# The first batch's last 64 queries as one step of their own, among the first group's products

## The chip, the cores and the metric

The kernel runs on one core of a Trainium2 chip. The metric is the device time of one execution in microseconds (us); the profiles are of one execution each, taken by the hardware profiler. Engines are named as in the profile: PE is TensorE's matrix multiplication, PEld its weight loads, DVE is VectorE, ACT ScalarE, POOL GpSimd, and SP issues most DMAs. TensorE has two clock levels, 1.2 and 2.4 GHz; the granted clock 1.00 in a row is the higher one.

## What is computed

Four batches of 8 heads with 576 queries and keys of width 64 go through attention in a causal window of 128 keys with a linear distance bias. The 2304 result rows go through a gated layer of width 1536, and then through 8 experts of width 1024, of which each row takes its best two by noisy logits. The core of the reference, cut:

```python
scores = scale * q @ k.T;  mask = (rel >= 0) & (rel < 128)
attn = softmax(where(mask, scores - slope[h] * abs(rel), -1e9)) @ v
g = x @ w_gate;  x = (silu(g) * (x @ w_val)) @ w_out
noisy = x @ g_w + log1p(exp(x @ n_w)) * noise      # best two of 8, softmax over the two
out[mask] += weight * (relu(x[mask] @ w1[e]) @ w2[e])
```

The weights of the gated layer come as 64-bit floats.

## The kernel before

**Order of the whole.** The attention of batch 0 runs first, alone. Then come four groups of result rows, `GRP`: rows 0 to 511, then 640, 512 and 640. For each group the gated layer (`mlp1`) is written as a list of pieces, `hidden` (12 blocks of 128 hidden units, two matrices, in halves) and `rows` (the product with `w_out`), and the attention of the next batch and small work on the last group (`post`) as a second list `side`. `merge(a, b, lead, late)` deals the second list evenly among the first, not before `late` pieces and not in the last `lead`. At the end come the routing (`route`) and the 8 experts.

**Who orders.** The instructions of each engine are put in order by a planner that simulates the program as written; within an engine they run in that order, each waiting for its semaphores. For DVE and POOL the first part of the program (until the sixth piece of the attention of batch 0) keeps the written order. So what is written later can be moved ahead: the conversion of the first weights (`Convert.one`, lines 224 to 238: ACT L232 and L233, DVE L234 and L235, a store to DRAM and the next load on SP) and their split into two rounded parts (ACT L280, DVE L281) lie between batch 0's attention. At most three split tiles (`wu`) and three converted ones (`wst`) can lie ready.

**Three products for one.** Every product of the gated layer is three matrix multiplications of rounded parts (`three`, L306 to L308). Its moving operand is `xT`, the attention result of a batch, channels on partitions.

**Group borders.** Batch 0 has 576 queries and group 0 takes 512 of them. The result of the last 64 goes to the tile `hold` and is copied in front of batch 1's result when batch 1's attention begins (`first`, L523). So it isn't needed before the second group.

**Attention of a pair of heads** (`pair_items`). Queries are cut into 9 blocks of 64. `tr` transposes q and k (`"t"`: the last 64 of both) and copies them to `qT` and `kT`; a score unit is one block of queries against up to 192 keys for two heads, 64 partitions each. In batch 0 (`qk1`, L427) q is laid out with zeros so that one multiplication over 128 rows gives both heads; the q copies are cut by head between ACT (L384) and DVE (L382), a call holds two units, and there are five calls. In the other batches (`qk4`, L444) four 64x64 tiles of TensorE work at once: two heads, two lanes of blocks; the second lane has its heads swapped on the partitions, and needs the bias table `tabs[1]`, which is `tabs[0]` shifted by 64 partitions. `softmax` adds the bias and takes the minimum of the negated scores (DVE L405), exponentiates (ACT L408), sums and inverts (L409, L410) and multiplies (POOL L417 in batch 0, DVE L415 in the others). `pt` transposes the probabilities (L461) and copies them (ACT L464 to L468, half-height ones on DVE L479 in batch 0). `pv` multiplies by v (L491) and writes the result in two rounded parts (ACT L507, DVE L508). The keys of `todo` give the order of a pair's pieces, and `z` shifts the pairs against each other.

**Buffers.** In batch 0 pairs 0 and 2 use one set (`SET[0]`), pairs 1 and 3 another that lies where the gated layer's hidden tiles come later. The other batches use `SET[0]` alone. Score banks are two, taken in turn by `qk1`.

**Constants.** `late_consts` (L646) issues `tabs[1]` on POOL and loads the routing weights and the noise on SP. It stands in front of the first group's products.

```python
bias(0)
...
late_consts()
...
    if b == 0:
        hidden.insert(3, lambda: (load_qk(1, 0), load_v(1, 0)))
```

## Time and profile before

| | us |
|---|---|
| median of 3 runs | 1104.43 (1102.92 to 1106.14) |
| the profiled execution | 1104.11 |
| its span, first to last instruction | 1102.0 |
| TensorE busy in the span | 1063.7 (97%) |
| DVE, ACT, POOL busy | 563.7, 476.4, 326.5 |
| mean granted clock | 0.987 |

A row that groups instructions reads: line, engine, operation, what is written from what, shapes, count, then busy us, mean ns of one, then idle time of the engine before them and what ended it. Instructions of one engine overlap at their ends, so a sum of durations can be over the time that passed; the distance from one start to the next is what counts there.

### The profile page before, as it was taken

The page shows a single profiled execution, that of the slowest core. Times are in us where ns is not written, and L with a number is a line of the kernel's source. Part 1 is how long each engine was busy: PE and PEld are TensorE (multiplying, and loading weights), DVE is VectorE, ACT ScalarE, POOL GpSimd, SP SyncE. Part 2 cuts the span into 40 slices and gives each one's busy share as a digit, 9 for nine tenths or more (in the row PEclk, how much of TensorE's full clock was granted, in tenths as well). Part 3 has the DMA queues.
Part 4 walks back from the last instruction along what each step waited for, and adds up shares of the span by engine and source line. Part 5 has one row for each costly group of instructions (what it writes and reads, how often), then busy time and mean ns, then how long its engine had stood idle before and what let it go on. Part 6 is the DMA issues. An engine that isn't in the chain of part 4 may idle for free. (4 is left out here: it accounts for less than half of the span.)

```text
span 1102.0 us, 17616 instructions
## 1 busy us (share of the span) xinstructions
PE 1063.7 (97%) x6694; PEld 909.1 (82%) x6694; DVE 563.7 (51%) x1267; ACT 476.4 (43%) x1093; POOL 326.5 (30%) x324
## 2 busy tenths in 40 slices
PE   6789999999999999999999999999999999999996
PEld 4457778799988777788998887988989898989894
DVE  6869972577640476325885355534343434343321
ACT  6868864566541456445543233423232323232210
POOL 5110003122223433142368324414141314141301
PEclk9889999999999999999999999999999999999998
DMA  8867664233362323241322415635353534443201
GB/s 208 224 202 236 218 223 154 73 91 90 101 231 82 122 86 110 71 153 39 99 96 96 153 40 165 201 113 174 105 173 105 173 115 153 136 154 115 71 27 42
DMA packets 124207, 143.87 MB, mean 131 GB/s; under 512 B 66062, under 2 KB 94766, under 8 KB 124112
## 3 DMA queue, kind: packets, MB, share of 16 engines
q1 hardware_dynamic: 112464, 108.88, 32.0%
q0 software_dynamic: 10448, 33.47, 9.1%
q8 instruction: 55, 0.90, 0.3%
q10 hardware_dynamic: 1200, 0.30, 0.1%
q14 instruction: 40, 0.33, 0.1%
HBM read 113.84 MB, written 28.91 MB: 130 GB/s over the span
## 5 line engine op out<-in xcount | busy, mean ns | idle before, releaser
L281 POOL TENSOR_TENSOR wu<-wst,wu 128x1024 fp32r<-128x1024 f32 x54 | 130.0, 2410 | 360.4 <-ACT wu L280 360.4
L910 PE MATMUL b<-xT,wu 128*128 128x304 f32 (+2 forms) x1536 | 221.4, 303 | 0.0
L910 PEld LDWEIGHTS b<-xT,wu 128*128 128x128 f32 x1536 | 216.5, 188 | 2.3 <-DVE xT L898 0.3
L306 PE MATMUL b<-xT,wu 128*128 128x320 f32 (+1 forms) x576 | 199.3, 350 | 0.8 <-ACT xT L507 0.8
L307 PE MATMUL b<-xT,wu 128*128 128x320 f32 (+1 forms) x576 | 196.2, 341 | 0.0
L308 PE MATMUL b<-xT,wu 128*128 128x320 f32 (+1 forms) x576 | 195.9, 341 | 0.0
L306 PE MATMUL b<-wu,hTa 128*128 128x512 f32 (+1 forms) x482 | 191.5, 400 | 0.2 <-DVE sg L590 0.2
L307 PE MATMUL b<-wu,hTa 128*128 128x512 f32 (+1 forms) x482 | 188.8, 392 | 0.0
L308 PE MATMUL b<-wu,hTa 128*128 128x512 f32 (+1 forms) x482 | 187.3, 392 | 0.0
L280 ACT ACTIVATE wu<-wst 128x1024 fp32r<-128x1024 f32 x136 | 143.6, 1058 | 95.4 <-PE b L308 72.1
L281 DVE TENSOR_TENSOR wu<-wst,wu 128x1024 fp32r<-128x1024 f32 x82 | 100.3, 1224 | 37.7 <-ACT wu L280 35.1
L306 PEld LDWEIGHTS b<-xT,wu 128*128 128x128 f32 x576 | 108.0, 189 | 13.4 <-issue 3.3
L917 DVE SCALAR_TENSOR_TENSOR hTa<-b,hTa 128x304 fp32r<-128x304 f32 (+2 forms) x128 | 56.8, 470 | 117.4 <-ACT hTa L916 101.4
L307 PEld LDWEIGHTS b<-xT,wu 128*128 128x128 f32 x576 | 108.5, 188 | 9.2 <-issue 1.7
L308 PEld LDWEIGHTS b<-xT,wu 128*128 128x128 f32 x576 | 108.5, 188 | 8.7 <-issue 1.5
L916 ACT ACTIVATE hTa<-b 128x304 fp32r<-128x304 f32 (+2 forms) x128 | 50.3, 422 | 145.6 <-PE b L910 140.0
L308 PEld LDWEIGHTS b<-wu,hTa 128*128 128x128 f32 (+1 forms) x482 | 88.9, 184 | 21.0 <-issue 0.3
L306 PEld LDWEIGHTS b<-wu,hTa 128*128 128x128 f32 (+1 forms) x482 | 88.8, 184 | 19.6 <-issue 1.5
L307 PEld LDWEIGHTS b<-wu,hTa 128*128 128x128 f32 (+1 forms) x482 | 89.0, 185 | 18.4 <-issue 0.2
L887 POOL DMA_INDIRECT xo<-x2d,gib x37 | 36.2, 980 | 174.4 <-PE b L894 164.0
L897 ACT ACTIVATE xT<-b 128x512 fp32r<-128x512 f32 (+1 forms) x40 | 22.9, 574 | 142.0 <-PE b L894 142.0
L592 DVE TENSOR_TENSOR hTa<-sg,hTa 128x320 fp32r<-128x320 f32 (+1 forms) x54 | 66.7, 1239 | 24.3 <-ACT hTa L591 24.3
(198 smaller groups left out, 1297.1 us busy)
## 6 DMA issues: line engine op xcount, KB each, us to landing
wst<-in_moe_w_dram SPq DMA_DIRECT2D x64, 512.0 KB, 3.7
wst<-wscr SPq DMA_DIRECT2D x54, 512.0 KB, 3.2
wscr<-wst SPq DMA_DIRECT2D x18, 512.0 KB, 3.1
cs<-in_moe_w_gate_dram SPq DMA_DIRECT2D x12, 512.0 KB, 4.8
cs<-in_moe_w_val_dram SPq DMA_DIRECT2D x12, 512.0 KB, 6.8
cs<-in_moe_w_out_dram SPq DMA_DIRECT2D x12, 512.0 KB, 5.7
x2d<-xT POOLq DMA_DIRECT2D x18, 256.0 KB
out_dram<-sg SPq DMA_DIRECT2D x1, 4608.0 KB, 15.6
```

Source lines behind the costliest of these rows:

```text
L280: nc.scalar.activation(o[0], s, AF.Copy)
L281: self.eng(n).tensor_sub(o[1], s, f32(o[0]))
L306: nc.tensor.matmul(ps, st(0), mv(0), start=first, stop=False, skip_group_check=True)
L307: nc.tensor.matmul(ps, st(0), mv(1), start=False, stop=False, skip_group_check=True)
L308: nc.tensor.matmul(ps, st(1), mv(0), start=False, stop=last, skip_group_check=True)
L592: nc.vector.tensor_sub(hh(1, f, sl), t, f32(hh(0, f, sl)))
L887: nc.gpsimd.indirect_dma_start(out=x[0:r], out_offset=None, in_=x2d[0:GRP[-1][0], :] if (e, g) == (0, False) else x2d, in_offset=bass.Indi ...
L897: nc.scalar.activation(d[0], tv, AF.Copy)
L910: nc.tensor.matmul(ps[g][:, 0:hi - lo], w[:, a, c * 128:(c + 1) * 128], xgt(e, m, g)[:, c, 0:hi - lo], start=(c == 0 and a + m == 0), stop ...
L916: nc.scalar.activation(d, ps[g][:, 0:hi - lo], AF.Relu)
L917: nc.vector.scalar_tensor_tensor(h2[1][:, f, lo:hi], ps[g][:, 0:hi - lo], 0.0, f32(d), op0=OP.max, op1=OP.subtract)
```

## The change

In batch 0 the pairs leave out block 8. The 64-row loads of q, k and v go, and the pieces `tr("t")`, the unit of block 8, `pt(4)` and the last part of the second `pv`. The eight other blocks go through `qk4` in two calls a pair, as in the other batches; the q layout with zeros, its memsets and the copies cut by head go. `tabs[1]` is therefore brought pair by pair, behind each call of `bias` (`swapped`, six POOL DMAs instead of two).

A new function `last` does block 8 for all 8 heads. It loads the last 64 queries, their 192 keys and values for all heads (five DMAs on SP), into `SET[0]`'s q, k and v tiles. `tr` transposes, `qk` makes 8 score products (two tiles at once), one `softmax` call takes four units with the multiplication on DVE, `pt` transposes the probabilities and copies them into the q and k tiles, and `pv` accumulates into one bank and writes `hold`. Its load is inserted in the pieces of the first group's products, its four steps stand first in `side`, then batch 1's first loads, `late_consts` and two empty entries; the side work begins after 6 pieces and not after 8.

```diff
+    def swapped(lo, hi):
+        for o in (0, QB):
+            nc.gpsimd.dma_start(tabs[1][o:o + QB, lo:hi], tabs[0][QB - o:128 - o, lo:hi])
+
     bias(0)
+    swapped(0, 1)
 
     def load_nat(t, src, b, p, rest=None):
 
         eng = nc.scalar if src is k and (b, p) == (0, 0) else nc.sync
         for i in range(2):
             eng.dma_start(t[:, 0:4, i, :], src[b, 2 * p + i, 0:512, :].rearrange("(i p) d -> p i d", p=128))
-        eng.dma_start(t[0:64, 4] if rest is None else rest, src[b, 2 * p:2 * p + 2, 512:576, :].rearrange("h p d -> p h d"))
+        if b:
+            eng.dma_start(t[0:64, 4] if rest is None else rest, src[b, 2 * p:2 * p + 2, 512:576, :].rearrange("h p d -> p h d"))
...
-                self.qt = self.r[:, 0:NQ * 128]
-
-            qv = self.qt.rearrange("p (j c) -> p j c", c=128)
-            nc.gpsimd.memset(qv[0:64, :, 64:128], 0.0)
-            nc.gpsimd.memset(qv[64:128, :, 0:64], 0.0)
...
-    PVS = [[(0, 0, 256, 0), (1, 0, 128, 128)],
-           [(1, 128, 128, 0), (2, 0, 256, 0), (3, 0, 192, 128), (4, 0, 64, 256)]]
+    def pvs(b, half):
+        if half == 0:
+            return [(0, 0, 256, 0), (1, 0, 128, 128)]
+        return [(1, 128, 128, 0), (2, 0, 256, 0)] + ([(3, 0, 192, 128), (4, 0, 64, 256)] if b else [(3, 0, 128, 128)])
...
+    def softmax(units, eng):
+
+
+        nu = len(units)
+        mn = att.tile([128, 5], F32, name="mn", bufs=4)
+        sm = att.tile([128, 5], F32, name="sm", bufs=4)
+        for i, (x, ps, tab) in enumerate(units):
+            nc.vector.tensor_tensor_reduce(x, ps, tab, op0=OP.add, op1=OP.min, scale=1.0, scalar=3e38,
+                                           accum_out=mn[:, i:i + 1])
+            nc.scalar.activation(x, x, AF.Exp, scale=-1.0, bias=mn[:, i:i + 1], accum_out=sm[:, i:i + 1])
+        nc.vector.tensor_scalar(sm[:, :nu], sm[:, :nu], 1e-9, None, op0=OP.add)
+        nc.vector.reciprocal(sm[:, :nu], sm[:, :nu])
+        for i, (x, _, _) in enumerate(units):
+            eng.tensor_scalar(x, x, sm[:, i:i + 1], 1.0, op0=OP.mult, op1=OP.mult)
...
+                                g, _, _, c = place(j)
+                                units.append((j % 8, (bf.s[g][:, c:c + w], ps[sw][:, po[sw]:po[sw] + w],
+                                                      tabs[sw][:, p, 192 - w:])))
                                 po[sw] += w
                     in_order(mm)
-                    softmax(sorted(units, key=lambda u: u[0] % 8))
+                    softmax([u for _, u in sorted(units, key=lambda u: u[0])], nc.vector if b else nc.gpsimd)
...
                     bias(p)
-
-            rest = lambda: (tr("t")(), nxt(load_qk))
+                    swapped(1, 2)
+
+            rest = lambda: (b and tr("t")(), nxt(load_qk))
             v0 = lambda: (vp(), pt(0)())
             if b == 0:
                 z = (0, 3, 7, 10)[p]
-                todo = [(0, first), (1, tr("k")), (2, rest), (3, qk1(0)), (4, qk1(1)), (5, qk1(2)), (6, v0), (7, qk1(3)),
-                        (7, pt(1)), (8, qk1(4)), (9, pv(0)), (10, pt(2)), (11, pt(3)), (12, pt(4)), (13, pv(1))]
+                todo = [(0, first), (1, tr("k")), (2, rest), (3, qk4((0, 1), (2, 3))), (5, qk4((4, 5), (6, 7))), (6, v0),
+                        (7, pt(1)), (9, pv(0)), (10, pt(2)), (11, pt(3)), (13, pv(1))]
...
+    def last(bk):
+
+        st = {}
+        bf = SET[0]
+
+        def load():
+            st["q"], st["k"] = bf.nat("qn"), bf.nat("kn")
+            t, m = slice(512, S), slice(384, 512)
+            for o, src, sl in ((st["q"][0:64], q, t), (st["q"][64:128], k, t), (st["k"], k, m), (bf.v[0], v, m),
+                               (bf.v[1][0:64], v, t)):
+                nc.sync.dma_start(o[:, 0:HP].rearrange("s p h d -> s (p h) d"), src[0, :, sl, :].rearrange("h s d -> s h d"))
+
+        def tr():
+            t = bk.get("t"), bk.get("t")
+            for i, src in enumerate((st["q"], st["k"])):
+                for p in range(HP):
+                    nc.tensor.transpose(t[i][:, p * 128:(p + 1) * 128], src[:, p].rearrange("s h d -> s (h d)"), ident)
+            t = [x.rearrange("c (p s) -> c p s", p=HP) for x in t]
+            st["qt"] = bf.qt[:, 0:256].rearrange("c (p s) -> c p s", p=HP)
+            st["kt"] = bf.qt[:, 256:1024].rearrange("c (p s) -> c p s", p=HP)
+            nc.scalar.activation(st["qt"], t[0][:, :, 0:64], AF.Copy, scale=-1.0 / math.sqrt(D))
+            nc.scalar.activation(st["kt"][:, :, 128:192], t[0][:, :, 64:128], AF.Copy)
+            nc.scalar.activation(st["kt"][:, :, 0:128], t[1], AF.Copy)
+
+        def x(p):
+            return bf.s[p // 2][:, p % 2 * 192:p % 2 * 192 + 192]
+
+        def qk():
+            ps = bk.get("s"), bk.get("s")
+            o = [ps[p // 2][:, p % 2 * 192:p % 2 * 192 + 192] for p in range(HP)]
+            for p in range(HP):
+                for h in range(2):
+                    hr = slice(64 * h, 64 * h + 64)
+                    nc.tensor.matmul(o[p][hr], st["qt"][hr, p], st["kt"][hr, p], start=True, stop=True, skip_group_check=True)
+            softmax([(x(p), o[p], tabs[0][:, p, :]) for p in range(HP)], nc.vector)
+
+        def pt():
+            t = bk.get("t"), bk.get("t")
+            for p in range(HP):
+                c = slice(p * 128, (p + 1) * 128)
+                nc.tensor.transpose(t[0][:, c], x(p)[:, 0:128], ident)
+                nc.tensor.transpose(t[1][0:64, c], x(p)[:, 128:192], ident)
+            st["p"] = [st["k"].rearrange("s i h d -> s (i h d)")[:, 0:512],
+                       st["q"].rearrange("s i h d -> s (i h d)")[0:64, 0:512]]
+            nc.scalar.activation(st["p"][0], t[0], AF.Copy)
+            nc.scalar.activation(st["p"][1], t[1][0:64], AF.Copy)
+
+        def pv():
+            o = bk.get("x")
+            mm = []
+            for p in range(HP):
+                for i, n in ((0, 128), (1, 64)):
+                    for h in range(2):
+                        mm.append(nc.tensor.matmul(
+                            o[64 * h:64 * h + 64, p * 64:(p + 1) * 64], bf.v[i][0:n, p, h, :],
+                            st["p"][i][:, p * 128 + h * 64:p * 128 + h * 64 + 64],
+                            start=(p == 0 and i == 0), stop=False, skip_group_check=True))
+            in_order(mm)
+            o = o[:, 0:256].rearrange("c (p s) -> c p s", p=HP)
+            nc.scalar.activation(hold[0][:, 0], o, AF.Copy)
+            nc.vector.tensor_sub(hold[0][:, 1], o, f32(hold[0][:, 0]))
+
+        return load, [tr, qk, pt, pv]
...
     def late_consts():
-        for o in (0, QB):
-            nc.gpsimd.dma_start(tabs[1][o:o + QB], tabs[0][QB - o:128 - o])
...
             bias(3)
+            swapped(2, 4)
...
-    late_consts()
     HT.append(main.tile([128, 2, NFA * GW], F32R, name="hTa"))
     HT.append(main.tile([128, 2, (NF - NFA) * GW], F32R, name="hTb"))
     ws.split(2)
@@ -991,12 +1031,14 @@
         side = (post(b - 1, std) if b else []) + attention(b + 1, std)
         hidden, rows = mlp1(b)
         if b == 0:
-            hidden.insert(3, lambda: (load_qk(1, 0), load_v(1, 0)))
+            load, tail = last(std)
+            side = tail + [lambda: (load_qk(1, 0), load_v(1, 0)), late_consts, lambda: None, lambda: None] + side
+            hidden.insert(2, load)
         if b == 1:
             merge(hidden, side)
             merge(rows, [zero_out])
         else:
-            merge(hidden + rows, side, 4, 0 if b else 8)
+            merge(hidden + rows, side, 4, 0 if b else 6)
```

## Rows read from the trace of the kernel before

**Rows 1.** Busy time by stretch; after the times: granted clock, DMA share, GB/s.

```profile
7.00:73.00 66.00, 51.59 (x286) 34.39 (x284) 50.01 (x189) 47.26 (x138) 18.32 (x44) 0.84 0.87 242
73.00:160.00 87.00, 86.79 (x529) 67.47 (x527) 76.29 (x151) 70.32 (x146) 0.74 (x2) 1.00 0.66 212
160.00:189.00 29.00, 28.00 (x143) 22.19 (x144) 8.83 (x26) 12.25 (x30) 5.62 (x4) 1.00 0.36 118
189.00:209.00 20.00, 17.89 (x171) 14.58 (x170) 9.31 (x39) 12.28 (x43) 3.83 (x4) 1.00 0.42 125
```

**Rows 2.** Groups of DVE instructions, 7 to 73 us.

```profile
L234 DVE SCALAR_TENSOR_TENSOR wst<-wst,cs 128x1024 int32<-128x1024 int32 x6 | 7.4, 1228 | 7.3 <-ACT cs L233 7.3
...
L405 DVE CUSTOM_DVE_ANT_0 sx<-b,tab 128x192 f32<-128x192 f32 (+2 forms) x18 | 5.3, 327 | 0.1
...
L479 DVE COPY xT<-b 64x128 f32<-64x128 f32 x16 | 4.5, 284 | 0.3 <-ACT xT L468 0.2
...
L409 DVE TENSOR_SCALAR sm<-sm 128x2 f32<-128x2 f32 (+1 forms) x20 | 3.5, 185 | 1.0 <-ACT sx L408 0.7 <-ACT hTb L408 0.3
...
L410 DVE RECIPROCAL sm<-sm 128x2 f32<-128x2 f32 (+1 forms) x20 | 2.9, 157 | 0.2
...
L382 DVE TENSOR_SCALAR qT<-b 64x512 f32<-64x512 f32 (+1 forms) x4 | 1.8, 461 | 4.1 <-ACT qT L384 4.0
```

**Rows 3.** Order of time on TensorE, around 189 to 209 us.

```profile
188.98 0.31 PE L306 MATMUL b<-xT,wu 128*128 128x320 f32 x1
...
205.86 1.03 PE L491 MATMUL b<-pt,v 128*64 128x128 f32 x16
```

**Rows 4.** Groups of ACT instructions, 7 to 73 us.

```profile
L408 ACT ACTIVATE sx<-sx,mn 128x192 f32<-128x192 f32 (+2 forms) x18 | 7.7, 432 | 3.3 <-DVE mn L405 2.1 <-DVE sm L410 1.1
...
L408 ACT ACTIVATION_READ_ACCUMULATOR sx<-sx,mn 128x1 f32 x18 | 3.5, 192 | 0.0
...
L507 ACT ACTIVATE hold<-b 128x64 fp32r<-128x64 f32 x3 | 0.6, 211 | 0.1
```

**Rows 5.** Groups of TensorE instructions, 7 to 73 us.

```profile
L427 PE MATMUL b<-hTa 128*128 128x192 f32 (+2 forms) x36 | 8.6, 370 | 4.1 <-DVE mn L405 4.1
L427 PE MATMUL b<-kT,qT 128*128 128x192 f32 (+2 forms) x36 | 7.4, 329 | 1.7 <-DVE mn L405 1.7
...
L461 PE MATMUL b<-ident,hTb 128*128 128x128 f32 (+1 forms) x26 | 6.1, 340 | 0.6 <-DVE xT L479 0.6
```

**Rows 6.** Groups of TensorE instructions, shapes apart, 73 to 189 us.

```profile
L444 PE MATMUL b<-kT,qT 64*64 64x192 f32 x84 | 5.6, 338 | 0.0
```

**Rows 7.** Order of time on TensorE: start, duration of the run, instructions.

```profile
52.52 0.33 PE L491 MATMUL b<-xT 64*64 64x64 f32 x4
52.78 0.55 PE L461 MATMUL b<-ident,sx 128*128 128x128 f32 x3
...
75.42 0.88 PE L444 MATMUL b<-kT,qT 64*64 64x192 f32 x20
76.23 0.50 PE L306 MATMUL b<-xT,wu 128*128 128x512 f32 x1
76.57 0.40 PE L307 MATMUL b<-xT,wu 128*128 128x512 f32 x1
76.81 0.39 PE L308 MATMUL b<-xT,wu 128*128 128x512 f32 x1
...
98.30 0.60 PE L363 MATMUL b<-ident,qn 128*128 128x128 f32 x4
98.83 0.66 PE L491 MATMUL b<-pt,v 128*64 128x128 f32 x8
```

**Rows 8.** Line 123, 0 to 75 us: issues (ns min/median/max), and time to landing.

```profile
L123 SPq DMA_DIRECT2D v<-in_v_dram x4: 601/640/1906, 7.6 to 66.9; - x4
...
DMA to landing us min/median/max: 2.3/2.4/5.3
```

**Rows 9.** Groups of POOL instructions, 0 to 73 us.

```profile
L647 POOL DMA_DIRECT2D tab<-tab x2 | 1.3, 674 | 0.4 <-DVE tab L113 0.4
```

More of the change, by code (lines that the diff above doesn't have):

```diff
@@ L166, in kt @@
         def kt(self):
-            return att.tile([128, S], F32, name="kT") if self.own else self.r[:, NQ * 128:NQ * 128 + S]
+            return att.tile([128, S], F32, name="kT") if self.own else self.r[:, S:2 * S]
     SET = {}
@@ L358, in go @@
                         st["k"] = bf.kt()
-                        st["q"] = (bf.qt if bf.own is False or b == 0 else bf.qt[:, 0:S])
+                        st["q"] = bf.qt[:, 0:S]
                     if what in "qk":
@@ L372, in go @@
                             nc.scalar.activation(st["k"][:, dst], t[:, so], AF.Copy)
-                        elif b:
+                        else:
                             nc.scalar.activation(st["q"][:, dst], t[:, so], AF.Copy, scale=sc)
-                        else:
-                            qv = st["q"].rearrange("p (j c) -> p j c", c=128)
-                            js = slice(dst.start // QB, dst.stop // QB)
-                            for h in range(2):
-                                pr = slice(64 * h, 64 * h + 64)
-                                o, x = qv[pr, js, 64 * h:64 * h + 64], t[pr, so].rearrange("p (j c) -> p j c", c=QB)
-                                if h:
-                                    nc.vector.tensor_scalar(o, x, sc, None, op0=OP.mult)
-                                else:
-                                    nc.scalar.activation(o, x, AF.Copy, scale=sc)
                 return go
@@ L484, in go @@
                     mm = []
-                    for n, (kb, so, w, c0) in enumerate(PVS[half]):
+                    for n, (kb, so, w, c0) in enumerate(pvs(b, half)):
                         kk = slice(0, 128 if kb < 4 else 64)
-                        cut = [so, so + w] if b == 0 or so >= 128 or so + w <= 128 else [so, 128, so + w]
+                        cut = [so, so + w] if so >= 128 or so + w <= 128 else [so, 128, so + w]
                         for lo, hi in zip(cut, cut[1:]):
-                            sw = (kb + lo // 128) % 2 if b else 0
+                            sw = (kb + lo // 128) % 2
                             for h in range(2):
@@ L499, in go @@
                         parts = [(0, w, xh[:, p, o + KEEP:o + KEEP + w], xl[:, p, o + KEEP:o + KEEP + w])]
-                    elif half == 0:
+                    elif half == 0 or b == 0:
+                        w = 256
                         parts = [(0, w, xh[:, p, o:o + w], xl[:, p, o:o + w])]
```

34 lines of the change are left out of this document (1 added, 33 removed).

## The prediction

> **What bounds the kernel now.** I read first the busy times by stretch [rows 1]. From 73 us TensorE is busy for 86.79 of 87 us, and until the end of the span it stays the engine that everything waits for (97% of the span by the page). Before 73 us it is not: in the 66 us from 7 to 73 TensorE is busy for 51.59 us, DVE for 50.01, ACT for 47.26, at a mean granted clock of 0.84 (between 1.2 and 2.4 GHz). None of them is full; the first batch's attention goes from one to the next and back, and the conversion of the first weights lies between. So there are two prices: work taken out before 73 us counts as far as the chain through the engines gets shorter, and TensorE work put in behind 73 us counts whole. The reader should next look at the row of L234 [rows 2]: DVE stood 7.3 us waiting for ACT's half of the conversion, with attention queued behind. And in 189 to 209 us [rows 1] TensorE is busy for 17.89 of 20 us: the first group's products end at 188.98 and the last pair of batch 1 only writes its result from 205.86 on [rows 3].
>
> **What goes from the stretch before 73 us.** DVE, durations from [rows 2]: four units of block 8 at 0.327 = 1.3 us; a softmax call now holds four units instead of two or one, so 2 calls a pair instead of 5, 12 of 20 sums (L409, 0.185) and 12 of 20 reciprocals (L410, 0.157) go = 4.1; the q copies of L382 all go, this row's 1.8 and as much for the other buffer set = 3.6; one of the eight L479 copies a pair, 4 x 0.284 = 1.1; four subtractions into hold, priced like ACT's 0.211 copy = 0.8. Together 10.9. ACT [rows 4]: four exponentials with their sums, 4 x (0.432 + 0.192) = 2.5; four 64-wide copies each of q, k and hold at 0.211 = 2.5; four copies after the transposes of block 8, priced like DVE's of the same tile at 0.284 = 1.1. Together 6.1. TensorE [rows 5]: the scores took 8.6 + 7.4 = 16.0 us in 72 passes; in the form of four tiles they are 128 passes, at batch 1's 5.6 / 84 = 0.067 [rows 6] that is 8.5, so 7.5 go; 4 + 8 transposes at 6.1 / 26 = 0.235 = 2.8; the last products with v, four times 0.33 [rows 7] = 1.3. Together 11.6. POOL's four multiplications, its four memsets of q and SP's issues of the 64-row loads (0.60 each [rows 8]) go too, and the three routing loads leave SP's queue; I price these at nothing, because TensorE, DVE and ACT are the fuller engines, and the loads of later pairs behind them on SP only come sooner.
>
> How much of it shortens the way to the first dense product? If ACT sets it, 6.1; if DVE does, 10.9; if all three shrink with their idle time, the saved 28.6 of 148.9 busy us, 19% of 66 = 12.7. None at all is excluded only in part: the conversions may fill what falls free, since they are ready to run. The work passes PE, DVE, ACT in turn, so I take the mean of the three savings, (10.9 + 6.1 + 11.6) / 3 = **9.5 us**. The bounds are 3 (half of ACT's) and 12.7.
>
> **What it costs there.** The second bias table, shifted by 64 partitions, now must be there for the first batch's second lane. It is brought by POOL DMAs, six instead of two at 0.674 each [rows 9], 2.7 us more on POOL, of which the memsets give back most; POOL's multiplications are queued behind them. A score unit of the second lane that waits for its table blocks DVE, with every later unit behind it. A DMA here lands 2.3 to 5.3 us after issue [rows 8]; bounds 0 and 5.3. The first pair's table is issued before its q and k are transposed, so I take the low side, **0.5 us**. The two score banks are now taken by one call at once, so the next call waits until DVE has read four units; in the rows before two calls overlapped, but there were five, so I leave it at nothing; uncovered it is under 1 us a call.
>
> **What is added behind 73 us.** The step for the last 64 queries has no cover on TensorE. Transposes: 8 of q and k, 8 of the probabilities; four take 0.53 us from start to the next start (98.30 to 98.83 [rows 7]), so 16 take 2.1. Scores: 4 pairs x 2 heads x 2 passes = 16 passes of 192 columns. Four tiles at once gave 20 passes in 0.81 us (75.42 to 76.23 [rows 7]), 0.040 each, as the low bound 0.65; one after another as in [rows 5], 16.0 / 72 = 0.22, as the high one 3.6. Two tiles are free of each other here, so twice the low one: 1.3. Products with v: 32 passes of 64 columns; four of that width took 0.26 us (52.52 to 52.78 [rows 7]), 0.065 each, 2.1, with bounds 1.3 (0.040) and 2.6 (0.083, the row's own 0.33 / 4). Each of the four returns to the products costs 0.1: the first product behind the scores holds the queue for 0.34 (76.23 to 76.57), the next for 0.24 [rows 7]: 0.4. Sum **5.9 us**, bounds 4.4 and 8.7.
>
> One rule of the Trainium skill speaks against the low prices: TensorEngine Tiling (Array Packing), Restrictions and Gotchas, says that different row tiles cannot access the same PSUM bank at the same time, and both heads of a pair write one bank here. By it the 16 passes would run one by one, 3.6 instead of 1.3, and the sum would be 2.3 us worse. The trace disagrees: batch 1's scores put two row tiles in each bank, and 20 passes in 0.81 us are five times faster than one by one.
>
> On DVE the step brings four units, one sum, one reciprocal, four multiplications and a subtraction, some 3.5 us by [rows 2], and on ACT as much and the copies. DVE is busy for 76.29 of 87 us in 73 to 160 [rows 1], which covers it while weights lie ready ahead; if that lead is used up, TensorE stands for up to these 3.5 us. In 160 to 189 DVE has 20 us free. I price it at nothing. The step's five loads on SP wait for buffers of pairs 0 and 2, and batch 1's first loads wait for its last product, since the probabilities lie in the q and k tiles; behind both on SP are the weight loads, covered by the same lead. The routing constants bring 3 issues and small POOL and DVE work, hidden by engines that have room (POOL is busy for 0.74 of 87 us).
>
> **The sum.** Against the profiled execution's own 1104.11 us (span 1102.0, so 2.1 around it): 1104.1 - 9.5 + 5.9 + 0.5 = **1101.0**. The median of the runs, 1104.43, lies 0.3 above that execution.
>
> **The rivals.** (1) *Batch 1 becomes late, slower.* Its side work began after 8 of the first group's 72 pieces; now the step and four entries stand ahead and it begins after 15. Seven pieces of six products at 0.24 are 10 us. If that carries through to the result at 205.86, the second group stands without input, for in 189 to 209 TensorE already has 2.1 us of idle: 1101.0 + 10 = 1111. It is slower than before from 3.1 us of lateness on. For it: the pairs share one buffer set and follow each other. Against: the free 20 us of DVE in 160 to 189, and the last pair's own place among the pieces is unchanged. (2) *The conversions fill the room.* ACT's saving alone counts, 6.1, because DVE keeps waiting in L234 and PE's saving is where it idled: 1104.1 - 6.1 + 5.9 + 0.5 = 1104.4, no change. For it: 7.3 us of such waits. Against: the conversions stop when their buffers are full. (3) *The idle time shrinks with the work.* 12.7 off, and the added step at its low bound: 1104.1 - 12.7 + 4.4 = 1095.8. For it: five calls a pair become two, each a round through three engines, and a low clock (0.84) in which less TensorE time counts double. Against: DMA is busy at 0.87 there [rows 1].
>
> **How the numbers follow.** The forecast's case, 1098 to 1103, has 0.38; (1) 0.15, (2) 0.26, (3) 0.21. A measurement of this kernel tells about 0.3%, 3.3 us, from no change, so faster is below 1101.1. The forecast lies on that edge; as its range reaches farther below, I give 0.27 of its 0.38 to faster and 0.11 to same. (3) is faster, (2) same with 0.24 and slower with 0.02, (1) slower with 0.13 and same with 0.02. That is 0.48 faster, 0.37 same, 0.15 slower. The range reaches from 1092 (rival 3 with the clock's help) to 1108 (rival 1 with two thirds of its lateness).
>
> **What would show it.** The first stretch of dense products should begin some 9 us before 73; at 68 or later the chain was ACT's (2). The first-batch scores should be quadrant tiles of 64x64. The step's own instructions should hold TensorE for about 6 us. The end of the first group's products should move from 189.0 to about 185.5, and all later stages by the same. DVE waiting for a table DMA before 15 us would show the 0.5 larger. The prediction is wrong if TensorE's idle time in the 20 us behind the first group's end grows beyond 2.1 us by more than 3, or if TensorE waits for a weight tile in the first group.

## The result, and the profile after

The changed kernel takes 1117.42 us (1115.94 to 1121.85, 4 runs) against 1104.45 of the kernel before: a ratio of 1.0124, 95% interval 1.0091 to 1.0156. The forecast was 1101.0. The profiled execution of the changed kernel took 1121.85 (span 1119.9), the longest of its four, so 17.9 us of span are to be explained here, and 13.0 between the medians; where the other 4.4 us of this execution lie, no second profile of it shows.

Three marks cut every profile into the same stretches: the end of the **first part** (DVE writes the last `xT` of batch 0, a 128x256 subtraction), the end of the **first group** (its successor's first product, 128x320), and the end of the span; 40 us behind the second mark are shown apart. First the kernel before, then the changed one, by these windows: times, then busy us of PE, PEld, DVE, ACT, POOL, then granted clock, DMA share, GB/s.

```profile
7.00:73.14 66.14, 51.73 (x286) 34.41 (x284) 50.01 (x190) 47.36 (x138) 18.32 (x44) 0.85 0.87 242
73.14:188.98 115.84, 114.63 (x670) 89.62 (x669) 85.11 (x176) 82.44 (x175) 6.34 (x6) 1.00 0.59 189
188.98:228.98 40.00, 37.89 (x354) 32.90 (x353) 22.83 (x71) 23.54 (x72) 9.45 (x7) 1.00 0.36 105
228.98:1102.00 873.02, 857.82 (x5382) 750.56 (x5382) 402.98 (x824) 321.30 (x708) 286.88 (x254) 1.00 0.36 115
```

```profile
7.00:77.75 70.75, 50.78 (x352) 32.39 (x352) 41.55 (x143) 44.29 (x116) 19.48 (x44) 0.76 0.79 213
77.75:198.79 121.04, 118.69 (x714) 92.12 (x710) 87.88 (x190) 83.44 (x181) 7.79 (x7) 1.00 0.61 191
198.79:238.79 40.00, 36.78 (x298) 30.40 (x297) 17.29 (x49) 21.18 (x64) 8.17 (x5) 0.87 0.34 93
238.79:1119.90 881.11, 865.37 (x5455) 757.05 (x5453) 410.10 (x846) 325.38 (x722) 288.02 (x255) 1.00 0.36 115
```

The first part is 4.6 us longer, the first group 5.2, the rest 8.1. In each row the length less the busy time is TensorE's idle time, and busy time times (1 - clock) is about what the lower clock takes. Worked out so, idle time grew by 5.6, 1.1, 1.1 and 0.5 = 8.3, the clock's part by 4.4 in the first part and 4.8 in the 40 us = 9.2, and the work at full clock by -5.4 in the first part and +5.7 behind it = 0.3. **The change moved work from one place to the other almost one for one; in this execution nearly the whole loss is idle time and clock.**

What the answers to [rows 2 to 5] show, 7 to 73 us: DVE's groups, then ACT's exponential on one of its two buffer sets, then TensorE's scores.

```profile
L237 DVE SCALAR_TENSOR_TENSOR wst<-wst,cs 128x1024 int32<-128x1024 int32 x6 | 7.5, 1254 | 9.8 <-ACT cs L236 9.8
...
L357 DVE CUSTOM_DVE_ANT_0 sx<-b,tab 128x192 f32<-128x192 f32 (+2 forms) x16 | 4.5, 322 | 6.2 <-PE b L418 5.3 <-PE b L437 0.9
...
L360 DVE TENSOR_SCALAR sm<-sm 128x4 f32<-128x4 f32 x8 | 1.3, 166 | 4.9 <-ACT sx L359 3.4 <-ACT hTb L359 1.5
```

```profile
L359 ACT ACTIVATE sx<-sx,mn 128x192 f32<-128x192 f32 (+2 forms) x16 | 6.8, 427 | 3.6 <-DVE mn L357 3.6
```

```profile
L418 PE MATMUL b<-hTa 64*64 64x192 f32 (+2 forms) x64 | 8.8, 498 | 9.2 <-DVE mn L357 5.2 <-DVE sm L360 4.0
...
L418 PE MATMUL b<-kT,qT 64*64 64x192 f32 (+2 forms) x64 | 6.1, 451 | 1.5 <-DVE sm L361 0.8 <-ACT qT L394 0.7
```

20 sums became 8, and 18 units in a row 16, as the diff says. But DVE now waits for the conversion's ACT half (9.8 us; 7.3 in [rows 2]), for TensorE's scores (6.2; 0.1 in [rows 2]) and for ACT's exponentials (4.9; 1.0), and TensorE waits 9.2 us for DVE ahead of the scores (4.1 in [rows 5]).

### The profile page after: what moved, and what is told of

It is laid out like the page before. It is cut to its first block, busy times and chain, and to the rows that moved or that the text cites. A ratio compares the mean times of both kernels' runs of the same rounds, so it can differ in the third digit from the quotient of the medians.

```text
span 1119.9 us, 17810 instructions
## 1 busy us (share of the span) xinstructions
PE 1073.1 (96%) x6818; PEld 913.5 (82%) x6818; DVE 559.0 (50%) x1234; ACT 476.0 (42%) x1083; POOL 327.3 (29%) x320
## 4 chain that ended last, share of the span: by engine, by line
PE 87%; DMA 4%; DVE 3%; ACT 3%; SPq 1%; issue 1%; POOL 1%; ACTq 0%; POOLq 0%; DVEq 0%
PE b L309 19%; PE b L311 19%; PE b L310 19%; PE b L950 19%; PE b L467 3%; PE b L437 2%; DMA cs<-in_moe_w_val_dram 2%; PE b L418 2%; PE b L934 1%; PE b L383 1%; ACT sx L359 1%; PE b L719 1%; PE b L732 1%; ACT wst L235 1%; DMA xo<-x2d,gib 0%
```

## The experiments

Where an experiment names the same edits as an earlier one, only what is new stands in the diff. The times and marks of all, in us (first part and first group end at the two marks; last pair: start of the last 16 products with v of batch 1, behind the first group's end):

```
kernel                 time      first part  first group  rest    last pair
before                 1104.45     73.1        115.8      913.0    16.9
changed                1117.42     77.8        121.0      921.1    24.9
e_nostep               1105.68     76.4        115.2      912.3    16.9
e_tabdve               1105.87     64.2        119.3      920.5    23.6
e_tabdve_timed         1106.15     66.7        120.8      919.2    23.8
e_tabearly             1114.18     71.4        120.0      920.9    21.6
e_oldscores            1109.02     68.1        120.0      919.1    24.7
e_scores               1112.74     79.5        116.0      915.4    19.3
e_scores_tabdve        1108.70     80.4        113.7      912.8    16.9
e_nostep_tabdve        1096.52     66.2        116.5      911.8    16.9
e_lead                 1105.69     65.1        134.5      904.3     6.5
e_own                  1122.14     76.8        123.9      922.6    22.7
e_own_tabdve           1112.69     66.3        124.4      920.1    21.7
e_mixed_late4          1103.74     64.9        126.3      914.8    19.3
e_mixed_lead12         1103.17     65.8        132.2      905.4    10.0
e_tabdve_lead8         1105.55     64.0        129.4      908.7    11.1
e_spread               1099.11     64.4        122.6      910.6    12.5
e_spread8              1098.93     65.9        125.5      907.6    10.8
e_spread_banks         1097.57     66.1        122.6      909.1    12.5
```

The runs from e_nostep to e_lead, without e_tabdve_timed, have a single time each and are compared by their marks, since single times of the kernel before lay between 1104.8 and 1110.4 beside them; the others are medians of 4 to 12 executions. The marks are of one profiled execution each, and those of one kernel differ: e_tabdve and e_tabdve_timed are the same program, with first parts of 64.2 and 66.7.

**Without the step.** Block 8 is left out for batch 0 and the kept columns are set to zero; batch 1's loads stand where they stood before.

```diff
-            load, tail = last(std)
...
-            hidden.insert(2, load)
+            nc.vector.memset(f32(hold[0][:, 0]), 0.0)
+            nc.vector.memset(f32(hold[0][:, 1]), 0.0)
+            side = [late_consts] + side
+            hidden.insert(3, lambda: (load_qk(1, 0), load_v(1, 0)))
```

> The changed kernel without its new step: block 8 of the first batch is left out, its result is zeros, and batch 1's first loads are issued as in the kernel before. Marks: the last result part of the first batch on DVE (73.14 us before, 77.75 changed), the second group's first product (188.98 and 198.79), batch 1's last product with v (205.86 and 223.65). Theory: the step makes the first group longer and batch 1 late. Then the first mark stays near 77, the distance to the second falls from 121 to 113 to 116, the third comes 17 us or less behind the second, and the time is 1104 to 1108 us. Rival: batch 1 is late because the first part of the kernel ends late and the conversions are pressed together. Then the third mark stays 22 us or more behind the second, and the time is 1111 us or more.

The first group and the rest go back to 115.2 and 912.3, the first part stays at 76.4. So the step costs 5.8 and 8.9 us behind the first part, 14.7 instead of the forecast's 5.9, and the first part is long from another cause.

**The shifted table on DVE**, and later the same timed.

```diff
-        for o in (0, QB):
-            nc.gpsimd.dma_start(tabs[1][o:o + QB, lo:hi], tabs[0][QB - o:128 - o, lo:hi])
+        for p in range(lo, hi):
+            for h in (2 * p, 2 * p + 1):
+                pr = slice((h + 1) % 2 * QB, (h + 1) % 2 * QB + QB)
+                nc.vector.scalar_tensor_tensor(tabs[1][pr, p, :], rel[pr], 2.0 ** (-8.0 * (h + 1) / H), big[pr],
+                                               op0=OP.mult, op1=OP.add)
```

> The changed kernel with the second table computed on DVE from the same distances (eight operations of 0.36 us more) in place of six POOL DMAs. Theory (table): the second lane's units no longer stand behind two conversions, the first mark falls from 77.75 to 69 to 73 us, the time to 1109 to 1113. Rival (calls of four units on both score banks, or the conversions, set the pace): the first mark stays at 76 to 80 us and the time at 1115 to 1120.

> The changed kernel with the shifted table computed on DVE, now timed in rounds. Theory: 1104-1108, the table's part of the loss is 11 us and what is left is the step's price. Rival (the one look was a chance of the planner's order, which is fixed, or of the chip): above 1110.

The first part falls by 13.5 us, to 64.2, more than was expected. Against the second profile of this kernel (66.7) it is 11.1, and by the medians, 1117.42 and 1106.15, 11.3; the ratio to before is 1.0001 (0.9984 to 1.0019). The row of e_tabdve's first part:

```profile
7.00:64.22 57.22, 44.22 (x363) 28.72 (x362) 43.92 (x153) 42.63 (x116) 16.03 (x38) 0.88 0.87 237
```

Beside the changed kernel's row, 7.0 of the 13.5 us are idle time of TensorE and 6.9 the clock (0.76 against 0.88): a late table is paid for twice. How the DMA cost that, the changed kernel's order of time shows: start, duration, then in brackets the idle time and its releaser. On DVE, then POOL, then TensorE:

```profile
13.10 0.17 DVE L360 TENSOR_SCALAR sm<-sm 128x4 f32<-128x4 f32 x1 [2.74 <-ACT sx L359]
...
13.40 2.52 DVE L113 SCALAR_TENSOR_TENSOR tab<-ra,rc 64x192 f32<-64x192 f32 x6
...
19.18 0.26 DVE L357 CUSTOM_DVE_ANT_0 hTb<-b,tab 128x128 f32<-128x128 f32 x1
...
20.87 1.27 DVE L237 SCALAR_TENSOR_TENSOR wst<-wst,cs 128x1024 int32<-128x1024 int32 x1 [1.43 <-ACT cs L236]
22.17 1.22 DVE L238 SCALAR_TENSOR_TENSOR wst<-cs,wst 128x1024 int32<-128x1024 int32 x1
...
28.80 1.23 DVE L238 SCALAR_TENSOR_TENSOR wst<-cs,wst 128x1024 int32<-128x1024 int32 x1
30.06 0.36 DVE L357 CUSTOM_DVE_ANT_0 hTb<-b,tab 128x192 f32<-128x192 f32 x1
```

```profile
13.72 2.00 POOL L363 TENSOR_SCALAR sx<-sx,sm 128x64 f32<-128x64 f32 x4 [5.85 <-DVE sm L361]
15.67 2.13 POOL L118 DMA_DIRECT2D tab<-tab  x4
```

```profile
30.75 1.54 PE L418 MATMUL b<-hTa 64*64 64x192 f32 x12 [4.41 <-DVE mn L357]
...
42.45 0.48 PE L418 MATMUL b<-hTa 64*64 64x64 f32 x4 [3.96 <-DVE sm L360]
```

DVE computes the other pairs' table (L113) behind the first softmax's sum, for which it waits until 13.10. POOL, in written order, multiplies first and issues the four table DMAs from 15.67 on. The second pair's first-lane units run at 18.93 and 19.18; its second-lane units need the table, stand in the order behind two conversions, and run at 30.06. TensorE waits for them at 30.75, and the next pair is late in turn. With the table on DVE the same two units follow at once:

```profile
18.96 0.26 DVE L360 CUSTOM_DVE_ANT_0 hTb<-b,tab 128x128 f32<-128x128 f32 x1
...
19.14 0.35 DVE L360 CUSTOM_DVE_ANT_0 hTb<-b,tab 128x192 f32<-128x192 f32 x1
```

**The table by DMA, but all of it early**: four `bias` and one `swapped(0, 4)` before any score.

```diff
-    bias(0)
-    swapped(0, 1)
+    for p in range(HP):
+        bias(p)
+    swapped(0, 4)
```

> The changed kernel with the biases of all four pairs written first, and the shifted table brought at once by two POOL DMAs before any score, in place of six spread ones. The marks (first mark: last result part of the first batch on DVE) were 77.75 us in the changed kernel, 64.22 with the second table computed on DVE. Theory (the place in the written order: biases stand behind the first softmax call, so the tables come late and the planner puts conversions ahead of the second lane's units): the first mark at 62 to 68 us, the time 1103 to 1108. Rival (a DMA for the table is late as such): the first mark at 74 us or later, the time 1114 or more.

Half comes back (71.4), which neither expectation had: 6.4 us were the place. DVE still waits for the DMA:

```profile
13.15 0.36 DVE L358 CUSTOM_DVE_ANT_0 sx<-b,tab 128x192 f32<-128x192 f32 x1 [3.60 <-DMA tab<-tab]
```

But this wait doesn't account for the 7.2 us that stay: the second pair's last units run at 24.41 here and at 24.49 with the table on DVE, so the lateness was made up by then, and what follows (the third pair's first unit at 31.43 against 27.80) was not taken apart.

**The scores alone.** First the changed kernel with the scores of before (`qk1`, calls of two, no second table in batch 0); then the kernel before with scores in four tiles and block 8 kept in the pairs; then that with the table on DVE. In the second, pairs 0 and 1 take pairs 2 and 3's probabilities for block 8, in the same amount of work.

```diff
 e_oldscores: -(3, qk4((0, 1), (2, 3))), (5, qk4((4, 5), (6, 7)))   +(3, qk1(0)), (4, qk1(1)), (5, qk1(2)), (7, qk1(3))
 e_scores:    -(3, qk1(0)), ..., (8, qk1(4))                        +(3, qk4((8, 0, 1), (2, 3))), (5, qk4((4, 5), (6, 7)))
```

> The changed kernel with the first batch's scores as in the kernel before (q laid out with zeros, calls of two units, one table); block 8 is still the new step. Theory (table): the first mark comes at 67 to 71 us, the first group is 119 to 122 us long, batch 1's last product 22 us or more behind it, and the time is 1108 to 1113. Rival (the conversions fill whatever falls free, so leaving out block 8 shortens nothing): the first mark at 73 us or later, the time 1114 or more.

> The kernel before with one part of the change: the first batch's scores as four tiles at once, block 8 in the first call of each pair as in the other batches, the shifted bias table brought pair by pair. No step. Theory (the second lane's units wait for the table, and weight conversions are put ahead of them): the first mark comes later than 73.14, at 75 to 80 us, and the time is 1106 to 1111. Rival (fewer and denser scores shorten the first part as predicted): the first mark at 66 to 70 us, the time 1097 to 1101.

> The kernel before with the first batch's scores as four tiles, block 8 kept in each pair (its transposes of probabilities moved ahead of the second pair's reuse of the buffer), the second table computed on DVE. No step. Theory (denser scores in two calls do shorten the first part once the table isn't waited for): first mark at 65 to 70 us, the rest as before, time 1096 to 1101. Rival (the shortening came only from leaving out block 8): first mark at 72 to 75, time 1103 to 1106.

Leaving out block 8 alone gives the first part 5.0 us (73.1 to 68.1); with it, the four tiles and the table on DVE give another 3.9 (64.2). But with block 8 kept the four tiles cost 6.3 and 7.3 us. Both expectations missed the last (80.4, for 65 to 70 or 72 to 75). There the way of the table makes no difference (79.5 by DMA, 80.4 on DVE), so the table's price belongs to the order of the changed kernel and not to the DMA alone. Fewer and larger calls are no gain by themselves; why they lose there (in the last, DVE stood 5.3 us for one conversion) stays open.

**No step, table on DVE; and the side work dealt earlier** (with the step). The first leaves block 8 out again.

```diff
 e_lead: -            merge(hidden + rows, side, 4, 0 if b else 6)
         +            merge(hidden + rows, side, *((4, 0) if b else (16, 4)))
```

> The second table computed on DVE, and no step: block 8 of the first batch is left out, its result is zeros, and batch 1's loads are issued as in the kernel before. It prices the step. Theory (the step costs its TensorE time in the first group, about 5 us, and makes batch 1 late, about 8): first mark 62 to 67 us, the first group 115 to 116 us long from there, 912 to 914 us from the second group's first product to the end; time 1090 to 1095. Rival (lateness comes from the earlier first mark, with fewer weights lying ready): the last part stays at 919 or more, time 1098 or more.

> The second table computed on DVE and the step kept, but in the first group the side work is dealt out earlier: it begins after 4 pieces and ends 16 before the last, not 6 and 4. Theory (the written place of batch 1's pieces sets how late they are): the stretch from the second group's first product to the end falls from 920.5 to 912 to 916 us, the time from 1105.9 to 1098 to 1102. Rival (the chain of the pairs through one buffer set, and full DVE and ACT, set it): the stretch stays within 2 us of 920.5 and the time at 1104 to 1108.

Without the step the marks come near the theory's, the time (1096.52) a little over it. So with the table on DVE the step costs 2.8 in the first group and 8.7 behind it. Dealt earlier, the rest falls to 904.3, but the first group grows by 15.2: what was lost moves, and the time stays.

**Tiles of its own for the step**, in `xT1`, which batch 1's result takes later, so that batch 1's loads no longer wait for the step's last product; with the table by DMA and on DVE.

```diff
-            st["q"], st["k"] = bf.nat("qn"), bf.nat("kn")
+            y = main.tile([128, 2 * KC * GW], F32, name="xT1")      # q, k, v, qt, kt and scores lie in y
+            hidden.insert(4, lambda: (load_qk(1, 0), load_v(1, 0)))
```

> The changed kernel, but the step for the last 64 queries has tiles of its own: they lie in the tile xT1, which batch 1's result takes only later. So batch 1's first loads of q, k and v no longer wait for the step's last product, and are issued two pieces behind the step's own. The shifted table still comes by POOL DMAs. Theory (the late stretch behind the first group comes from batch 1's pairs starting late, because their buffers were the step's): the rest behind the first group's end falls from 921.1 us to 911-915, the first part stays at 76-79, the first group at 118-121, the time is 1107-1112. Rival (the step's own work on DVE, ACT and TensorE makes batch 1 late, whatever its buffers): the rest stays at 918-922 and the time at 1114-1119.

> The same, and the shifted table computed on DVE. Theory: the two costs lie in different stretches and add up: first part 64-67 us, first group 117-120, rest 911-915, so 1094-1100, faster than both kernels. Rival (the step's own work makes batch 1 late): rest 918-922 and 1102-1107, no faster than the kernel before. Second rival (the first part's gain is given back as soon as batch 1 is early, because the weights' conversion then is the bound of the first group): first group over 123, time over 1101.

Both theories missed: ratios to before of 1.0137 (1.0106 to 1.0167) and 1.0053 (1.0038 to 1.0068), slower, and the rest is unchanged. (The second rival's numbers came out, but the first group is as long, 123.9, where the table came by DMA and there was no gain to give back.) `xT1` is free only at the end of the first part, so the step's loads start at 76.45 and not at 25.7, and batch 1's first transposes stand in the order right behind the step's last products:

```profile
111.62 2.18 PE L582 MATMUL b<-xT 128*64 128x64 f32 x32
113.73 0.66 PE L383 MATMUL b<-ident,qn 128*128 128x128 f32 x4
```

So this did not test the buffers alone. What it did show is the same low clock in the same place; the changed kernel has it here, TensorE's order of time and then windows of 4 us:

```profile
211.55 0.67 PE L437 MATMUL b<-ident,sx 128*64 128x128 f32 x2 [1.24 <-DVE sx L363]
212.80 0.90 PE L437 MATMUL b<-ident,sx 128*128 128x128 f32 x3 [0.58 <-DVE sx L363]
...
214.69 0.69 PE L437 MATMUL b<-ident,sx 128*128 128x128 f32 x2 [0.36 <-ACT pt L453]
...
223.65 1.03 PE L467 MATMUL b<-pt,v 128*64 128x128 f32 x16
```

```profile
206.79:210.79 4.00, 2.93 (x39) 1.87 (x35) 2.87 (x21) 3.46 (x15) 0.00 (x0) 1.00 0.70 161
210.79:214.79 4.00, 2.30 (x10) 1.21 (x11) 2.58 (x14) 2.32 (x11) 0.00 (x0) 0.52 0.00 0
214.79:218.79 4.00, 4.00 (x20) 3.19 (x21) 0.42 (x1) 2.03 (x7) 0.00 (x0) 0.50 0.02 4
218.79:222.79 4.00, 4.00 (x25) 3.34 (x24) 1.46 (x3) 1.31 (x5) 0.00 (x0) 0.70 0.00 0
```

Between 203.17 and 216.91 us TensorE runs steps of pairs 2 and 3 of batch 1 and small transposes, with three products of the gated layer among them. It stands in several short waits, each for the next step. The granted clock is 1.00 until 210.79 us, with 1.07 us of idle time in the 4 us before, and falls inside the wait of 1.24 us:

```profile
210.79:211.79 1.00, 0.24 (x2) 0.18 (x2) 0.96 (x7) 1.00 (x6) 0.00 (x0) 0.57 0.00 0
```

It stays at 0.5 (1.2 GHz) until about 221, though TensorE is busy without a break from 215 on. By the order as written, seven dependent steps of pair 3 (transposes, scores, products with v) stand with nothing dense between them. (Eleven of pair 2 stand so behind the first group's product 342; there 0.7 us were idle and the clock stayed.)

The order alone doesn't decide it. In the kernel before, five such steps stand together behind the first group; in e_scores, which has no new step, the same five stand with the same waits. First the kernel before, where the clock stayed, then e_scores, where it fell (the last line of each is the row of a window, in which the third number from the end is the clock):

```profile
199.22 0.55 PE L461 MATMUL b<-ident,sx 128*128 128x128 f32 x3 [1.57 <-ACT pt L477]
...
200.68 0.44 PE L461 MATMUL b<-ident,sx 128*128 128x128 f32 x2 [0.54 <-ACT pt L477]
...
201.00:205.00 4.00, 4.00 (x34) 3.03 (x33) 1.40 (x3) 3.04 (x11) 0.00 (x0) 1.00 0.02 4
```

```profile
205.74 0.55 PE L453 MATMUL b<-ident,sx 128*128 128x128 f32 x3 [1.57 <-ACT pt L469]
...
207.20 0.63 PE L453 MATMUL b<-ident,sx 128*128 128x128 f32 x2 [0.54 <-ACT pt L469]
...
207.30:210.70 3.40, 3.40 (x18) 2.64 (x19) 0.42 (x1) 1.63 (x6) 0.00 (x0) 0.50 0.00 0
```

What the runs show is how often it comes. Of the nine profiles with the step in the changed kernel's order, seven have a low clock in the 40 us behind the first group (0.87 to 0.96), and the two in which the side work ends earlier (e_lead, and e_tabdve_lead8 below) have it in the first group. Of the five without the step, one has it.

**The last pair moved**, three ways, all with the table on DVE. The first two let the step's four pieces alternate with the first three of batch 1 (probabilities, scores, v and the transposed q and k of the step in `xT1`, the loaded q and k where they were), so that its chain and batch 1's run side by side; they differ in where the side work starts and ends. The third changes only the dealing.

```diff
 e_mixed_late4:  side = [tr, batch 1's loads, first, qk, k, pt, rest, pv, late_consts, ...]; merge(..., 4, 4)
 e_mixed_lead12: the same;                                                                  merge(..., 12, 4)
 e_tabdve_lead8: the order of the changed kernel;                                           merge(..., 8, 4)
```

> The changed kernel with the shifted table computed on DVE; the step keeps the q and k tiles for its loads only, and has its probabilities, scores, transposed q and k and v in the tile xT1 (free until batch 1's result), batch 1's first loads stand behind the step's transposes, the step's four pieces alternate with the first three of batch 1, and the copy of the kept columns moves behind them; the side work begins after 4 pieces. In the order of TensorE's instructions batch 1's last pair then stands where it stood in the kernel before (its q transposes behind 358 products of the first group, its first scores behind 441; in the changed kernel behind 430 and 456, with nothing dense between its steps). Theory (what costs behind the first group is the place of the last pair: standing close together it leaves TensorE idle, and the clock falls): rest 911-915 with no low clock in the 30 us behind the first group, first part 64-68, first group 117-122, time 1094-1101. Rival (the step's own work or batch 1's late start costs the 8 us wherever the last pair stands): rest 918-922 and 1103-1108.

> The same, but the side work ends 12 pieces before the end of the first group's list: the last pair then stands at 342 to 432 products, inside the first group. Theory: its products are done under the first group, so the rest falls to 903-908 and the first group grows to 124-129 by the pair's own products and no more; time 1094-1101, with no low clock on either side. Rival (the wait only moves, as with the earlier lead of 16): first group over 131 with idle time and a low clock inside, time 1104 or more.

> The changed kernel with the table on DVE; of the step nothing is changed, only that the side work begins after 4 pieces and ends 8 before the end. The last pair then stands at 342 to 418 products with dense products between, but pairs 2 and 3 meet at 342. Theory: behind the first group no idle time and no low clock, rest 904-910; at the meeting place in the first group some idle time, first group 125-131; time 1098-1105. Rival (late start decides): 1105-1109 as with the earlier lead of 16.

The first two were faster than before, 0.9975 (0.9958 to 0.9993) and 0.9969 (0.9950 to 0.9988), the third no different, 0.9993 (0.9974 to 1.0013). The rest fell in all three, as expected, but the first group grew, in the first two beyond the ranges (126.3 and 132.2), and the third's time, 1105.55, lies in its rival's range: pair 2 and, in the second and third, pair 3 now stood close around product 342, TensorE waited there, and the clock fell there in all three. In the first it fell again behind the first group (0.50 from 203.83 to 207.24). So the loss moves with the place where steps stand together, which none of the three was free of. Of the first, around that place:

```profile
162.00:166.00 4.00, 2.36 (x25) 1.11 (x15) 3.01 (x16) 2.43 (x10) 0.00 (x0) 1.00 0.35 78
166.00:170.00 4.00, 3.91 (x15) 2.58 (x16) 1.36 (x6) 2.43 (x9) 0.00 (x0) 0.57 0.00 0
```

Not all of its 126.3 us is this. The profiled execution, 1107.9 us, is the longest of its twelve, and its first group began at a low clock that the first part had left, which takes some 2.9 us:

```profile
64.92:70.92 6.00, 5.97 (x21) 4.48 (x23) 2.94 (x4) 4.01 (x8) 0.00 (x0) 0.52 0.85 248
```

**Steps spread.** The order is that of e_mixed_late4, but batch 1's pairs are written 9 keys apart (e_spread) or 8, with the side work ending 8 pieces before the end (e_spread8). Both were chosen from the order of instructions alone, so that no more than four dependent steps stand together.

```diff
 e_spread:  -  z = p * 10      +  z = p * (10 if b > 1 else 9);   merge(..., 4, 4)
 e_spread8: -  z = p * 10      +  z = p * (10 if b > 1 else 8);   merge(..., 8, 4)
```

> The same with 8 keys between the pairs and the side work ending 8 pieces before the end: the pairs overlap more, the last pair stands at 376 to 454 products. Theory: no low clock either, the first group 120-125 and the rest 906-911; time 1093-1100. Rival (the low clock comes in whatever order): 1101-1106.

With 9 keys 1099.11, ratio 0.9946 (0.9932 to 0.9961); with 8 keys 1098.93 (1097.68 to 1100.87), ratio 0.9943 (0.9930 to 0.9956): faster than both kernels, as expected, with first groups a little over the ranges expected (118 to 122 and 120 to 125). In both the clock is 1.00 from the first group to 40 us behind it. With 8 keys TensorE idles 1.06 and 0.20 us there:

```profile
7.00:65.92 58.92, 43.42 (x345) 28.32 (x343) 42.96 (x148) 41.71 (x113) 16.04 (x38) 0.88 0.88 235
65.92:191.38 125.46, 124.40 (x790) 96.87 (x791) 94.67 (x221) 92.28 (x214) 8.19 (x7) 1.00 0.63 196
191.38:231.38 40.00, 39.80 (x338) 36.13 (x336) 22.67 (x56) 21.60 (x65) 10.30 (x6) 1.00 0.37 106
231.38:1099.00 867.62, 851.76 (x5342) 745.01 (x5340) 398.92 (x808) 317.78 (x694) 284.63 (x253) 1.00 0.37 115
```

TensorE's busy time behind the first part is 1016.0 here, against 1010.3 before: 5.6 us, the step's own work.

**Four score banks** in the first batch, with pairs 9 keys apart (e_spread with two banks: 1099.11).

```diff
-    pro = Banks([2, 3], [4, 5], [6, 7])
+    pro = Banks([2, 3, 0, 1], [4, 5], [6, 7])
```

> As e_spread (pairs 9 keys apart), but the first batch's scores take four banks in turn instead of two (the two added ones are those of the first group's products), so a call no longer waits until the call before has been read. The forecast left that wait at nothing, under 1 us a call. If nothing is right: first part 63-66 us as before, time within 2 us of the kernel with two banks, 1097-1101. If the wait counts, up to 1 us for each of 7 later calls: first part 58-62, time 1092-1096. If the first group's products, which now share these banks, start later for it: first part the same, first group over 124, time above 1101.

1097.57, ratio 0.9928 (0.9913 to 0.9942), an interval that overlaps those of the two spread kernels; the first part stays (66.1), so the banks were no bound there.

## Why the prediction was wrong, step by step

- **The saving of 9.5 us in the first part** came out near once the table is there in time: 73.1 to 64.2 is 8.9 (6.4 by the kernel's second profile). But this is luck in part, for the terms that it is the mean of were too large. With the table on DVE, TensorE's busy time fell 7.5 (11.6 forecast), DVE's 6.1 with the new table's work in it (10.9) and ACT's 4.7 (6.1), a mean of 6.1; the lower clock took 2.5 us less than before, which no term of the sum had. Of TensorE's, the scores miss most: with the table on DVE they take 5.3 + 4.9 = 10.2 us in 128 passes, 0.080 each, where 0.067 from [rows 6] gave 8.5, and in the changed kernel, at a clock of 0.76, 8.8 + 6.1 = 14.9.

```profile
L421 PE MATMUL b<-hTa 64*64 64x192 f32 (+2 forms) x64 | 5.3, 398 | 2.4 <-DVE mn L360 2.4
...
L421 PE MATMUL b<-kT,qT 64*64 64x192 f32 (+2 forms) x64 | 4.9, 386 | 0.9 <-ACT qT L397 0.7 <-DVE mn L360 0.2
```

- **"I take the low side, 0.5 us"** for the shifted table is the step that failed first; it cost 13.5 by these profiles and 11.3 by the medians. The forecast asked when a DMA lands, with 5.3 as its upper bound. It did not ask when the DMA is issued, namely behind POOL's multiplications (it had them the other way round), or what the planner puts on DVE meanwhile: conversions of 2.5 us each (1.27 + 1.22), behind which a late unit then stands. Its own sign for this, DVE waiting for a table DMA before 15 us, doesn't show in the changed kernel: the first pair's table is there in time, and in front of the second's units DVE has other work. This term alone turns the sum into 1114; the profiled 1121.85 are 7.8 more, nearly all from behind the first part (13.3 us instead of 5.9 there, the third and fourth point).
- **5.9 us of TensorE work for the step** was right: 5.7 in the changed kernel and 5.6 in the spread one. Scores held TensorE for 1.45 us (77.21 to 78.66; 1.3 forecast), the products with v for 2.1 (91.57 to 93.67; 2.1 forecast). By the bank rule of the Trainium skill (TensorEngine Tiling (Array Packing), Restrictions and Gotchas) the scores would have held it for 3.6; the trace disagrees again, with two row tiles in one bank.
- **"I price it at nothing"** for batch 1's lateness failed as well, and rival 1 named the place: the last pair's last products start 24.9 us behind the first group instead of 16.9 [rows 3], 8.0 late for the rival's 10. It came on top of the other failure. But its price is not the idle time that the rival worked with. That grew by only 1.0 in the 20 us behind the group, under the 3 that the forecast set as its sign; of the 8.1 us behind the group 4.8 went to the clock, 1.6 to idle time, and 1.7 is work that now lies behind the mark.
- **Rival 2** was close in kind: DVE waited 9.8 us in the conversion. But it named no term by which the first part could grow. **Rival 3** has no run for it: the first part's idle time, 14.4 us before, is 13.0 at the least of all runs (e_tabdve) and 15.5 in e_spread8 (58.92 less 43.42).
- **Two score banks at nothing, and the routing constants hidden**: the banks hold (66.1 against 64.4 to 65.9 with two); nothing contradicts the second, which no run tested alone.

## What to carry to other kernels

A step that only waits for a small copy is not priced by the copy's latency: ask which queue issues it, what stands ahead there, and what the consumer's engine will have been given to do by the time it lands. Work moved under a busy engine is better written so that its dependent steps have dense work between them: the same step cost 11.4 to 14.7 us with its neighbours bunched and 4.7 to 4.8 spread (first group and rest, against the kernels without it; the spread kernels also have tiles of their own for the step and deal its pieces in turn with batch 1's, so the spreading wasn't priced alone). The order of instructions shows where steps stand together before any run, but not whether the clock will fall there. When time is lost, split each stretch into work, idle time and clock before looking for causes.

## What the runs showed of the hardware

- A copy of 64 partitions within SBUF, issued by POOL, landed in a median of 5.5 us; L118 of the changed kernel:

```profile
DMA to landing us min/median/max: 4.2/5.5/5.8
```

  Six of the eight DVE instructions that take its place in e_tabdve needed 0.83 + 1.45 = 2.3 us.
- Short waits of TensorE, none over 1.6 us, were followed by half the clock on busy time: in the changed kernel the granted clock fell to 0.5 at about 211 us with 1.07 us of idle time in the 4 us before, and stayed there to about 221. The same waits don't always do it: 1.57 and 0.54 us left the clock at 1.00 in the kernel before and were followed by 0.50 in e_scores. In the changed kernel this took 4.8 us, more than the idle time that had grown. Where the limit lies, these runs do not tell.
